# Scores in two PSUM banks with the last 128 keys of two heads in a common bank, four common banks instead of two, spread directly ahead of the values, and the first chunk's split moved into the attention

## The chip, the cores and the metric

The kernel runs on one core of one Trainium2 chip. The metric is the device time of one execution in microseconds. Engines: TensorE (PE), VectorE (DVE), ScalarE (ACT), GpSimd (POOL), and SyncE (SP), which issues most DMAs. Each engine executes its own instructions in a fixed order; semaphores make one wait for another. PSUM has eight banks of 512 float32 per partition.

## What is computed

```python
q_pool = q.reshape(B, H, S // 2, 2, D).mean(axis=3)      # B 2, H 8, S 1152, D 64
scores = q_pool @ k.transpose(0, 1, 3, 2) / sqrt(D)
attn = exp(scores - max(scores)); attn /= attn.sum(-1) + 1e-9
x = (attn @ v)                                           # as 1152 tokens x 512
x = softplus(x @ w_in) @ w_out                           # d_ff 2048
out = max(x @ w1, x @ w2, x @ w3) @ w_out2               # d_ff 768
```

The dense weights arrive as float64 and are turned to float32 on the chip. Where a product must be more exact than one float32r matmul, an operand is split into a high and a low part, and two or three matmuls are summed.

## The kernel before, in words

The sixteen heads are worked on in eight pairs (`pr`). A pair has 1152 keys and 576 pooled queries a head: four query tiles of 128 for each head (`t` 0 to 3, `i` the head) and one tile that holds the last 64 queries of both heads, nine tiles in all (`one_tile`, L588).

One tile goes through five steps. `scores` (L437) fills a score tile of three PSUM banks, 384 keys in each, with two matmuls a bank (three for the ninth tile). `key_max` (L453) takes the negated maximum of all 1152 scores on DVE. `exps` (L459) makes the exponentials on ACT with that maximum as bias, in one instruction, and its accumulator gives the row's sum. `turn_e` (L472) transposes them on PE, 3 x 128 keys at a time, into one of two common banks, and `keep_e` (L478) copies that bank to SBUF as `p`, on ACT or DVE as the table `ENGINE` says (D or A for each third of each tile). There are two score tiles, six banks, and two common banks (`NTB`). The common banks also serve the transposes of k and q for the next pair (`turn_k`, `turn_q`), the spread inverses and the values.

After four (or five) tiles `finish` (L614) adds the second half: `inverse` (L496) makes 1 / sum on DVE, `spread` (L505) turns it along the columns on PE, `keep_spread` (L530) copies it to `rr` on ACT, `values` (L518) multiplies p by v in 36 matmuls, and `divide` (L541) multiplies both into `xy` on DVE.

The order of all this is not the order of the code. `Order` (L47) collects every step with an engine, a cost, a place, what it reads and writes, and whether it takes or frees a common bank. `ordered` then plays the steps through with those costs, always taking on an engine the step with the lowest place that could start, and the result is the instruction order of every engine. Places are the tile's number plus an offset from the table `AT` or, for the next pair's preparation, `PREP`. Ten dense weights are prepared in gaps of the last pairs (`load_weight` on SP, `size_weight` on ACT, `bound_weight` on POOL, `float_weight` in three steps on DVE, `high_weight` on ACT, `low_weight` on DVE).

The dense part has an `Order` of its own (L692), on seven of the eight banks, over three chunks of 384 tokens. `halves_x` (L875) splits a chunk: `high_x` (L783) casts on ACT and `low_x` (L786) subtracts on POOL, in four pieces. `up` (L714) is one projection of 12 matmuls; `size_h`, `lost1`, `lost2`, `log_h`, `lost3`, `soft`, `high_g`, `low_g` make the softplus and its split on ACT, DVE and POOL; `down` (L760) follows four projections later. Line names in the trace: s is a score tile, nm the negated maximum, te the transposed exponentials, tk and tq transposed k and q, tr the spread inverses, x under L522 the values, bank_h, bank_y, bank_o the dense banks.

Of the kernel before, what the change touches and what calls it, by code (L numbers as in the profile page):

```python
# [124 lines left out]
def kernel(  # L130
# [52 lines left out]
    xy = xpool.tile([P, NC, NTOK], F32, tag="xy", name="xy")  # L183
    pools = {"pre": wpre}
# [252 lines left out]
    def scores(m, pr, i, t, b):  # L437
        if b == 0:
            tiles["s", m] = ps.tile([P, NB, 512], F32, tag=slot("s", m, NS), name=f"s_{m}")
        sp = tiles["s", m]  # L440
        q1, q2, k1, kl = q1s[pr % 2], q2s[pr % 2], tiles["k1", pr], tiles["kl", pr]
        cols = slice(b * BK, (b + 1) * BK)
        to = sp[:, b, :BK]
# [9 lines left out]
    def key_max(m):  # L453
        tiles["nm", m] = sm.tile([P, 1], F32, tag=slot("nm", m, 3), name=f"nm_{m}")
# [4 lines left out]
    def exps(m, w, x, first):  # L459
        e = pp.tile([P, S], F32, tag=slot("e", m, NE), name=f"e_{m}")  # L460
        if first:
            tiles["sum", w] = sm.tile([P, 5], F32, tag=slot("sum", w, 2), name=f"sum_{w}")
        nc.scalar.activation(  # L463
            out=e.rearrange("p (b s) -> p b s", b=NB),
            in_=tiles["s", m][:, :, :BK],
            func=AF.Exp,
            bias=tiles["nm", m],
            accum_out=tiles["sum", w][:, x : x + 1],
        )
        tiles["e", m] = e  # L470
# [22 lines left out]
    def width(w):  # L493
        return 2 * QB if w % 2 == 0 else 2 * QB + TAILQ

    def inverse(w):  # L496
# [3 lines left out]
        nc.vector.tensor_scalar(  # L500
            out=r[:, :nx], in0=tiles["sum", w][:, :nx], scalar1=1e-9, scalar2=None, op0=ALU.add
# [28 lines left out]
    def keep_spread(w, n):  # L530
        rr = sm.tile([P, 2 * QB + TAILQ], F32, tag="rr", name=f"rr_{w}")
        tiles["rr", w] = rr
        nc.scalar.copy(rr[:, : width(w)], tiles["t", n])

    def token_cols(w):
# [3 lines left out]
        return c, slice(t0, t0 + width(w))  # L539

    def divide(w, n):  # L541
        c, cols = token_cols(w)
        nc.vector.tensor_tensor(
            out=xy[:, c, cols], in0=tiles["t", n], in1=tiles["rr", w][:, : width(w)], op=ALU.mult
        )

    counts = {"t": 0}
    TILES = 2 * NT + 1

# [37 lines left out]

    def one_tile(pr, x):  # L588
        i, t = (x % 2, x // 2) if x < 2 * NT else (0, NT)
        m = TILES * pr + x  # L590
        w = 2 * pr + (t >= 2)
# [3 lines left out]
        banks = [f"{s}_{b}" for b in range(NB)]  # L595
        for b in range(NB):
            order.add("PE", 0.35 if t < NT else 0.52, m + b / NB, scores, m, pr, i, t, b,
                      reads=[f"q{z}{y}_{g}" for z in (1, 2) for g in range(2)]
                      + [f"q1{y}_d0", f"q1{y}_d1", f"k1{y}_0{b}", f"k1{y}_1{b}", f"kl{y}_{b}"],
                      writes=(banks[b],) + ((s,) if b == 0 else ()))  # L600
        order.add("DVE", 1.28, m + AT["max"], key_max, m, reads=banks + [s], writes=(slot("nm", m, 3),))
        order.add("ACT", 1.21, m + AT["exp"], exps, m, w, sx, sx == 0,
                  reads=[slot("nm", m, 3), s] + banks, writes=(e, f"sum{w % 2}"))
        for b in range(NB):
            n, p = next_bank(), m + AT["turn"] + b / NB
            engine = ENGINE[sx][b]
            order.add("PE", 0.33, p, turn_e, m, b, n, reads=(e, "pw"), writes=(f"b{n}",), take=("t", n))
# [6 lines left out]
    def finish(m, w):  # L614
        nx = 4 if w % 2 == 0 else 5
        y = (w // 2) % 2
        at = m + AT["values"]
        n1, n2 = next_bank(), next_bank()
        order.add("DVE", 0.3, m + 0.3, inverse, w, reads=(f"sum{w % 2}",), writes=(f"r{w % 2}",))
        order.add("PE", 0.6, m + AT["spread"], spread, w, n1, reads=(f"r{w % 2}",), writes=(f"b{n1}",), take=("t", n1))  # L620
        order.add("ACT", 0.36, m + AT["spread"], keep_spread, w, n1, reads=(f"b{n1}",), writes=("rr",), free=("t", n1))
        order.add("PE", 4.0 if w % 2 == 0 else 4.9, at, values, w, n2,
                  reads=[f"p_{x}_{b}" for x in range(nx) for b in range(NB)] + [f"v{y}"],
                  writes=(f"b{n2}", "pw"), take=("t", n2))
        order.add("DVE", 0.4, at - 3, divide, w, n2, reads=(f"b{n2}", "rr"), free=("t", n2))
# [40 lines left out]
    FIRST = (2, 3, 4, 5, 6, 7, 1)  # L666
# [13 lines left out]
    def tok(ch):  # L680
        return slice(ch * TOK, (ch + 1) * TOK)


    xs = {}
    for ch in reversed(range(NCH)):
# [97 lines left out]
    def high_x(ch, c):  # L783
        nc.scalar.copy(xs[0, ch][:, c], xy[:, c, tok(ch)])

    def low_x(ch, c):  # L786
        nc.gpsimd.tensor_tensor(
            out=xs[1, ch][:, c],
# [209 lines left out]
```

## Time and profile before

| | us |
|---|---|
| median of 3 runs (lowest, highest) | 676.99 (676.8, 677.45) |
| span of the profiled execution | 675.7 |
| difference of the median to that span | 1.3 |
| PE matmul busy in it | 637.5 (94%) |
| PE weight loads busy | 556.3 (82%) |
| DVE, ACT, POOL busy | 446.9, 351.5, 219.6 |

For the profiled execution the profile gives the span, from its first to its last instruction; some 1.3 us lie around it, as the third line has it. Busy shares are means over stages that have different limits: the attention runs to about 308.8 us, the dense layers from there to the end. A matmul's row ends when its last result is modelled to have left the array, so the rows of neighbours overlap, and the distance of their starts tells what one costs.

### The profile page before, as it was taken

Reading aid. Unit: us, or ns where it says so; the run is one execution under the profiler, and the core shown is the slowest. Engines: PE = TensorE matmul, PEld = TensorE weight load, DVE = VectorE, ACT = ScalarE, POOL = GpSimd, SP = SyncE. Lnnn points to the kernel's source line nnn. Section 1 sums busy time; section 2 is a strip of 40 time slices with the busy share of each in tenths; the row PEclk is TensorE's granted clock in tenths of the full one; section 3 lists DMA queues with packets and bytes.
Section 4 is the critical chain, followed back from the end, with each engine's and each line's share of the span. In section 5 each row is a group of like instructions: output and inputs, shape, how many; then the busy total and the mean of one; then the engine's idle time right before and its main releaser. Section 6 shows DMA issues by size and latency. Waiting matters only on the chain.

```text
span 675.7 us, 10352 instructions
## 1 busy us (share of the span) xinstructions
PE 637.5 (94%) x3914; PEld 556.3 (82%) x3914; DVE 446.9 (66%) x747; ACT 351.5 (52%) x697; POOL 219.6 (32%) x204
## 2 busy tenths in 40 slices
PE   2899999999999998999899999999999999999997
PEld 1676677676767766667799999999999999999996
DVE  3866667667777799985867979797688871111111
ACT  4655555556565666656767676767574431211211
POOL 1100000000000112216987877779695510000000
PEclk9999999999999999999799999999999999999999
DMA  7443433324241735212223333232022310100101
GB/s 191 107 105 89 96 98 73 100 69 98 68 99 43 198 116 164 94 64 81 76 63 97 122 98 122 94 126 93 32 94 95 124 32 1 47 1 1 47 1 48
DMA packets 56546, 56.87 MB, mean 84 GB/s; under 512 B 21168, under 2 KB 47792, under 8 KB 56496
## 3 DMA queue, kind: packets, MB, share of 16 engines
q1 hardware_dynamic: 55280, 55.62, 28.8%
q10 hardware_dynamic: 1216, 0.59, 0.3%
q8 instruction: 31, 0.51, 0.3%
q14 instruction: 19, 0.16, 0.1%
HBM read 43.52 MB, written 2.36 MB: 68 GB/s over the span
## 4 chain that ended last, share of the span: by engine, by line
PE 78%; DVE 10%; ACT 6%; issue 2%; DMA 2%; POOL 2%; SPq 0%; ACTq 0%; DVEq 0%; POOLq 0%
PE bank_h_m L675 17%; PE bank_h L675 15%; PE bank_y L675 14%; PE x L522 9%; PE te L476 7%; PE bank_o L675 6%; DVE nm L455 4%; PE s L446 4%; ACT e L463 4%; DVE p L491 3%; PE s L447 3%; DMA k<-in_k_dram 2%; ACT p L489 1%; PE tk L348 1%; PE s L449 1%
## 5 line engine op out<-in xcount | busy, mean ns | idle before, releaser
L226 POOL TENSOR_SCALAR size<-size 128x512 f32<-128x512 f32 x56 | 84.3, 1507 | 98.9 <-ACT size L221 98.7
L675 PE MATMUL bank_h_m<-x,wh 128*128 128x384 f32 x432 | 114.6, 339 | 0.0
L476 PE MATMUL te<-ident,e 128*128 128x128 f32 x648 | 101.8, 282 | 11.2 <-DVE p L491 7.8
L455 DVE TENSOR_REDUCE nm<-s 128x1 f32<-128x1152 f32 x72 | 97.4, 1352 | 14.7 <-PE s L447 12.5
L675 PE MATMUL bank_h<-x,wh 128*128 128x384 f32 x384 | 106.3, 339 | 0.2 <-DVE gl L757 0.2
L476 PEld LDWEIGHTS te<-ident,e 128*128 128x128 f32 x648 | 73.1, 140 | 38.8 <-DVE p L491 20.1
L463 ACT ACTIVATE e<-s,nm 128x1152 f32<-128x1152 f32 x72 | 88.3, 1226 | 22.0 <-DVE nm L455 17.0
L675 PEld LDWEIGHTS bank_h_m<-x,wh 128*128 128x128 f32 x432 | 78.9, 188 | 0.8
L446 PE MATMUL s<-k,q 128*128 128x384 f32 x192 | 76.1, 396 | 3.1 <-ACT e L463 3.1
L489 ACT COPY p<-te 128x384 f32<-128x384 f32 x88 | 39.7, 482 | 72.0 <-PE te L476 71.8
L491 DVE COPY p<-te 128x384 f32<-128x384 f32 x128 | 66.5, 552 | 11.7 <-PE te L476 9.9
L522 PE MATMUL x<-p,v 128*64 128x320 f32 (+1 forms) x576 | 73.3, 408 | 0.0
L675 PE MATMUL bank_h_m<-x,wl 128*128 128x384 f32 x216 | 73.1, 338 | 0.0
L675 PEld LDWEIGHTS bank_h<-x,wh 128*128 128x128 f32 x384 | 70.3, 188 | 1.1 <-DVE gl L757 0.6
L675 PE MATMUL bank_y<-gh,wh 128*128 128x384 f32 x192 | 66.1, 344 | 3.7 <-ACT gh L752 3.7
L333 POOL TENSOR_TENSOR qs<-q 128x512 f32<-128x512 f32 x7 | 8.9, 1273 | 185.7 <-PE tq L401 166.5
L675 PE MATMUL bank_y<-gl,wh 128*128 128x384 f32 x192 | 65.9, 343 | 0.1
L675 PE MATMUL bank_y<-gh,wl 128*128 128x384 f32 x192 | 65.8, 343 | 0.0
L447 PE MATMUL s<-kl,q 128*128 128x384 f32 x192 | 65.4, 341 | 0.0
L675 PE MATMUL bank_h<-x,wl 128*128 128x384 f32 x192 | 65.0, 339 | 0.0
L522 PEld LDWEIGHTS x<-p,v 128*64 128x64 f32 x576 | 39.9, 137 | 28.2 <-issue 2.3
L733 POOL TENSOR_TENSOR d<-e,d 128x384 f32<-128x384 f32 x48 | 49.0, 1022 | 29.1 <-DVE d L726 26.5
(216 smaller groups left out, 1096.9 us busy)
## 6 DMA issues: line engine op xcount, KB each, us to landing
raw<-in_moe_w_out_dram SPq DMA_DIRECT2D x22, 512.0 KB, 3.3
raw<-in_moe_w_dram SPq DMA_DIRECT2D x18, 512.0 KB, 3.5
raw<-in_moe_w_in_dram SPq DMA_DIRECT2D x16, 512.0 KB, 3.8
k<-kh SPq DMA_DIRECT2D x28, 288.0 KB, 5.8
k<-in_k_dram SPq DMA_DIRECT2D x16, 288.0 KB, 4.5
v<-in_v_dram SPq DMA_DIRECT2D x16, 288.0 KB, 3.2
q<-in_q_dram SPq DMA_DIRECT2D x14, 256.0 KB, 3.2
out_dram<-ob SPq DMA_DIRECT2D x9, 256.0 KB, 2.0
```

What stands on the lines that cost most here:

```text
L226: nc.gpsimd.tensor_scalar(out=size, in0=size, scalar1=SMALLEST, scalar2=None, op0=ALU.max)
L333: engine.tensor_tensor(out=qs.rearrange("p t i d -> p i t d"), in0=q1[:, :, :, 0], in1=q1[:, :, :, 1], op=ALU.add)
L446: nc.tensor.matmul(to, q1[:, i, at1 : at1 + QB], k1[:, i, cols], start=True, stop=False)
L447: nc.tensor.matmul(to, q2[:, at2 : at2 + QB], kl[:, cols], start=False, stop=True)
L455: nc.vector.tensor_reduce(out=tiles["nm", m], in_=tiles["s", m][:, :, :BK], axis=AX.XY, op=ALU.max, negate=True)
L463: nc.scalar.activation(out=e.rearrange("p (b s) -> p b s", b=NB), in_=tiles["s", m][:, :, :BK], func=AF.Exp, bias=tiles["nm", m], accum_ou ...
L476: nc.tensor.transpose(tp[:, t], tiles["e", m][:, j * P : (j + 1) * P], ident)
L489: nc.scalar.copy(to, tp)
L491: nc.vector.tensor_copy(to, tp)
L522: nc.tensor.matmul(x[halves(i)], tiles["v", w // 2][:, i, j], tiles["p", w, j // KT][:, i, j % KT, : width(w)], start=(j == 0), stop=(j == ...
L675: nc.tensor.matmul(ps, lhs(a, kk), rhs(bb, kk), start=start and n == 0, stop=stop and n == last)
L733: nc.gpsimd.tensor_tensor(out=d, in0=gs["e", i], in1=d, op=ALU.subtract)
```

## The change

- A score tile has two banks of 512 keys (`SB`). The last 128 keys of both heads of a query tile go to one common bank, `rest_scores`, and have their own maximum, `rest_max`; `key_max` takes the maximum of the 1024 and then the minimum of the two negated maxima. `exps` covers 1024 keys and `rest_exps` the last 128; each accumulates its own sum, and `inverse` adds the two.
- The freed two banks become common banks: `NTB` is 4.
- The spread is placed directly ahead of the values and waits for the same copies; `rr` has two buffers.
- For chunk 0 the casts and subtractions of `halves_x` are made in the attention, one piece after each of the first four pairs; its two tiles are allocated at the start.
- The tables `AT`, `ENGINE` and `PREP` have new numbers, and the planner's costs are those of the new steps. The dense part takes its banks in another order (`FIRST`).

```diff
-NTB = 2
+NTB = 4
-AT = {"max": -1.78, "exp": -0.31, "turn": 0.93, "keep": 0.1, "spread": 4.0, "values": 5.26}
-ENGINE = ["DAA", "DDD", "DAA", "DDA", "ADD"]
-PREP = {1: -5.28, 2: -7.74, 3: -4.5, 4: -3.31, 5: -1.64}
+SB = 512
+AT = {"rest": -0.7, "max": 2.3, "exp": -0.95, "turn": 1.03, "keep": -0.1, "values": 4.27}
+ENGINE = ["DAA", "DAD", "DAA", "DAD", "ADA"]
+PREP = {1: -2.9, 2: -10.61, 3: -7.52, 4: -3.98, 5: -5.52}
...
+    def scores(m, pr, i, t, b):
+        if b == 0:
+            tiles["s", m] = ps.tile([P, NM, SB], F32, tag=slot("s", m, NS), name=f"s_{m}")
+        score(tiles["s", m][:, b], pr, i, t, slice(b * SB, (b + 1) * SB))
+
+    def rest_scores(w, pr, t, n):
+        tp = bank(n, [P, heads(t), NR], f"sr_{w}")
+        for i in range(heads(t)):
+            score(tp[:, i], pr, i, t, slice(NM * SB, S))
+
+    def rest_max(w, t, n):
+        tiles["nr", w] = sm.tile([P, 2], F32, tag=slot("nr", w, 2), name=f"nr_{w}")
         nc.vector.tensor_reduce(
-            out=tiles["nm", m], in_=tiles["s", m][:, :, :BK], axis=AX.XY, op=ALU.max, negate=True
-        )
+            out=tiles["nr", w][:, : heads(t)], in_=tiles["t", n], axis=AX.X, op=ALU.max, negate=True
+        )
+
+    def key_max(m, w, i):
+        nm = sm.tile([P, 2], F32, tag=slot("nm", m, 3), name=f"nm_{m}")
+        nc.vector.tensor_reduce(out=nm[:, 1:], in_=tiles["s", m], axis=AX.XY, op=ALU.max, negate=True)
+        nc.vector.tensor_tensor(out=nm[:, :1], in0=nm[:, 1:], in1=tiles["nr", w][:, i : i + 1], op=ALU.min)
+        tiles["nm", m] = nm[:, :1]
...
+    def rest_exps(m, w, sx, i, n):
+        nc.scalar.activation(
+            out=tiles["e", m][:, NM * SB :],
+            in_=tiles["t", n][:, i],
+            func=AF.Exp,
+            bias=tiles["nm", m],
+            accum_out=tiles["sum", w][:, 1, sx : sx + 1],
+        )
...
+        if i == 0:
+            n = rests[u] = next_bank()
+            p = m + AT["rest"]
+            order.add("PE", 0.44 if t < NT else 0.33, p, rest_scores, u, pr, t, n,
+                      reads=qs + ks(NM * SB, S), writes=(f"b{n}",), take=("t", n))
+            order.add("DVE", 0.3 if t < NT else 0.2, p, rest_max, u, t, n, reads=(f"b{n}",), writes=(f"nr{u % 2}",))
...
+        order.add("ACT", 0.31, m + AT["exp"], rest_exps, m, w, sx, i, n, reads=[nm, f"b{n}"],
+                  writes=(e + "r", f"sum{w % 2}"), free=("t", n) if i == heads(t) - 1 else None)
...
-        order.add("PE", 0.6, m + AT["spread"], spread, w, n1, reads=(f"r{w % 2}",), writes=(f"b{n1}",), take=("t", n1))
-        order.add("ACT", 0.36, m + AT["spread"], keep_spread, w, n1, reads=(f"b{n1}",), writes=("rr",), free=("t", n1))
+        order.add("PE", 0.7 if w % 2 == 0 else 0.9, at - 0.01, spread, w, n1, reads=[f"r{w % 2}"] + ready,
+                  writes=(f"b{n1}",), take=("t", n1))
+        order.add("ACT", 0.4, at - 3, keep_spread, w, n1, reads=(f"b{n1}",), writes=(f"rr{w % 2}",), free=("t", n1))
...
+        if w % 2 and w // 2 < NC:
+            order.add("ACT", 0.46, at, high_x, 0, w // 2, reads=(f"x{w - 1}", f"x{w}"), writes=(f"xh{w}",))
+            order.add("POOL", 1.1, at, low_x, 0, w // 2, reads=(f"xh{w}",))
...
-        if f == 0:
-            halves_x(ch, at - 6 if i else -100)
+        if f == 0 and i:
+            halves_x(ch, at - 6)
```

The new tables move instructions on every engine. Two places show it. The first is PE in a steady pair, behind the shorter value block (the last six of its 18 matmuls stand in the first row; s is a score tile, te a third of the transposed exponentials of one tile). Before:

```order
L522 MATMUL x_1140<-p_2_1011,v_662 64x256 x6
L476 MATMUL te_0_1169<-ident,e_1052 128x128 x3
L449 MATMUL s_1126<-k_2_799,q_0_97 128x384
L450 MATMUL s_1126<-k_2_799,q_0_97 128x384
L451 MATMUL s_1126<-kl_735,q_0_98 128x384
L476 MATMUL te_1_1179<-ident,e_1052 128x128 x3
L476 MATMUL te_2_1185<-ident,e_1052 128x128 x3
L476 MATMUL te_0_1193<-ident,e_1080 128x128 x3
L476 MATMUL te_1_1199<-ident,e_1080 128x128 x3
L476 MATMUL te_2_1205<-ident,e_1080 128x128 x3
L476 MATMUL te_0_1209<-ident,e_1112 128x128 x3
L476 MATMUL te_1_1217<-ident,e_1112 128x128 x3
```

In the changed kernel the transposes behind the same block, from the fifth row behind it on, read (sr is the common bank of the rest scores):

```order
L494 MATMUL te_2_1265<-ident,e_1153 128x128 x3
L494 MATMUL te_0_1272<-ident,e_1184 128x128 x3
L494 MATMUL te_1_1278<-ident,e_1184 128x128 x3
L443 MATMUL s_1282<-k_2_799,q_0_99 128x512
L444 MATMUL s_1282<-k_2_799,q_0_99 128x512
L445 MATMUL s_1282<-kl_611,q_0_100 128x512
L494 MATMUL te_2_1294<-ident,e_1184 128x128 x3
L494 MATMUL te_0_1300<-ident,e_1245 128x128 x3
L443 MATMUL sr_1305<-k_2_799,q_0_99 128x128
L444 MATMUL sr_1305<-k_2_799,q_0_99 128x128
L445 MATMUL sr_1305<-kl_611,q_0_100 128x128
```

Before, nine groups of transposes, seven of which stand here, follow one another with no score matmul between; now two or three groups alternate with half a score tile or a rest tile.

The second place is ACT at the junction of attention and dense layers: rr is the last copy of spread inverses, x the cast halves of a chunk (x_0, x_1, x_2 in the first block are chunks 0, 1, 2), wh and size belong to weights, e and u to the softplus of the first projection. Before:

```order
L533 COPY rr_3176<-tr_3150 128x320
L784 CAST x_0_3209<-xy 128x384 x4
L784 CAST x_1_3207<-xy 128x384
L265 CAST wh_3224<-t_3212 128x512
L221 ACTIVATE size_3227<-raw_3059 128x512
L784 CAST x_1_3207<-xy 128x384 x3
L784 CAST x_2_3205<-xy 128x384 x3
L265 CAST wh_3259<-t_3232 128x512
L221 ACTIVATE size_3262<-raw_3222 128x512
L784 CAST x_2_3205<-xy 128x384
L720 ACTIVATE e_3282<-bank_h_3242 128x384
L721 ACTIVATE e_3282<-e_3282 128x384
```

In the changed kernel:

```order
L555 COPY rr_3450<-tr_3424 128x320
L572 CAST x_1_3481<-xy 128x384 x4
L572 CAST x_2_3479<-xy 128x384
L261 CAST wh_3522<-t_3497 128x512
L768 ACTIVATE e_3525<-bank_h_3483 128x384
L769 ACTIVATE e_3525<-e_3525 128x384
L785 ACTIVATE u_3532<-e_3525 128x384
L217 ACTIVATE size_3550<-raw_3403 128x512
```

The casts of chunk 0 are gone from here, and the softplus of the first projection stands behind one weight cast instead of two weight casts, two sizes and seven casts of x that follow the fifth.

## Rows read from the trace of the kernel before

**Rows 1.** Windows: span, busy us (instructions) of PE, PEld, DVE, ACT, POOL; clock, DMA.
```profile
38.20:76.00 37.80, 35.29 (x251) 26.34 (x250) 25.72 (x39) 19.82 (x40) 1.68 (x2) 1.00 0.36 87
...
183.03:218.59 35.56, 34.18 (x246) 25.44 (x245) 24.71 (x38) 19.88 (x38) 1.68 (x2) 1.00 0.32 76
218.59:255.97 37.38, 34.72 (x249) 25.92 (x248) 31.58 (x51) 24.46 (x47) 6.28 (x5) 1.00 0.57 156
255.97:288.99 33.02, 30.62 (x223) 22.55 (x222) 32.62 (x54) 21.61 (x41) 8.80 (x6) 1.00 0.41 117
288.99:303.82 14.83, 13.35 (x104) 9.30 (x104) 11.80 (x20) 8.41 (x16) 3.37 (x2) 1.00 0.20 72
...
308.80:331.00 22.20, 18.17 (x88) 16.84 (x87) 18.48 (x31) 15.70 (x33) 17.30 (x17) 0.85 0.30 96
```

**Rows 2.** Critical chain: start us, us, what ran.
```profile
...
183.10 4.04 PE x L522 x36
199.70 5.00 PE x L522 x36
...
506.81 2.12 PE bank_h L675 x12
...
540.71 2.11 PE bank_o L675 x9
```

**Rows 3.** Timeline of PE, 187 to 199 us: start us, us, instruction.
```profile
187.98 0.84 PE L476 MATMUL te<-ident,e 128*128 128x128 f32 x6
...
191.49 1.67 PE L476 MATMUL te<-ident,e 128*128 128x128 f32 x9 [0.19 <-DVE p L491]
192.91 0.42 PE L446 MATMUL s<-k,q 128*128 128x384 f32 x1
...
193.59 0.42 PE L446 MATMUL s<-k,q 128*128 128x384 f32 x1
...
194.27 0.42 PE L446 MATMUL s<-k,q 128*128 128x384 f32 x1
```

**Rows 4.** Lines of DVE, 183.03 to 218.59 us: busy us, mean ns, idle before.
```profile
L455 DVE TENSOR_REDUCE nm<-s 128x1 f32<-128x1152 f32 x9 | 12.2, 1352 | 2.0 <-PE s L447 2.0
L491 DVE COPY p<-te 128x384 f32<-128x384 f32 x16 | 8.3, 552 | 1.4 <-PE te L476 1.1
...
L543 DVE TENSOR_TENSOR xy<-x,rr 128x320 f32<-128x320 f32 x1 | 0.5, 493 | 2.4 <-PE x L522 2.4
L543 DVE TENSOR_TENSOR xy<-x,rr 128x256 f32<-128x256 f32 x1 | 0.4, 425 | 3.0 <-PE x L522 3.0
...
L503 DVE RECIPROCAL r<-r 128x4 f32<-128x4 f32 x1 | 0.2, 178 | 0.0
```

**Rows 5.** Lines of ACT, the same stretch.
```profile
L463 ACT ACTIVATE e<-s,nm 128x1152 f32<-128x1152 f32 x9 | 11.0, 1223 | 3.1 <-DVE nm L455 2.8 <-PE te L476 0.2
L489 ACT COPY p<-te 128x384 f32<-128x384 f32 x11 | 4.9, 480 | 10.9 <-PE te L476 10.9
L463 ACT ACTIVATION_READ_ACCUMULATOR e<-s,nm 128x1 f32 x9 | 1.8, 195 | 0.0
...
L417 ACT ACTIVATE q<-tq 64x64 fp32r<-64x64 f32 x2 | 0.4, 211 | 0.0
```

**Rows 6.** Timeline of all engines, 308.9 to 324 us.
```profile
311.01 0.70 DVE L250 SCALAR_TENSOR_TENSOR t<-raw,t 128x512 int32<-128x512 int32 x1
...
312.80 2.57 ACT L784 CAST x<-xy 128x384 fp32r<-128x384 f32 x6
...
316.80 0.50 ACT L720 ACTIVATE e<-bank_h 128x384 f32<-128x384 f32 x1
...
323.29 0.69 PE L675 MATMUL bank_y<-gh,wh 128*128 128x384 f32 x1 [3.67 <-ACT gh L752]
```

**Rows 7.** Timeline of PE, 324 to 332 us.
```profile
324.91 0.52 PE L675 MATMUL bank_y<-gh,wh 128*128 128x384 f32 x1
325.23 0.52 PE L675 MATMUL bank_y<-gh,wl 128*128 128x384 f32 x1
```

More of the change, by code (lines that the diff above doesn't have):

```diff
@@ L183 @@
     xy = xpool.tile([P, NC, NTOK], F32, tag="xy", name="xy")
+    xs = {(z, 0): xpool.tile([P, NC, TOK], F32R, tag=f"x{z}0", name=f"x_{z}_0") for z in range(2)}
     pools = {"pre": wpre}
@@ L435, in both_q, with score @@
         nc.sync.dma_start(q1[D:, 1, TAILQ:], q2[D:, NQ:])
[L437 to L440, printed above, removed]
+    NM = S // SB
+    NR = S - NM * SB
+    def score(to, pr, i, t, cols):
         q1, q2, k1, kl = q1s[pr % 2], q2s[pr % 2], tiles["k1", pr], tiles["kl", pr]
-        cols = slice(b * BK, (b + 1) * BK)
-        to = sp[:, b, :BK]
         if t < NT:
@@ L463, in exps @@
+    def exps(m, w, sx):
+        tiles["e", m] = pp.tile([P, S], F32, tag=slot("e", m, NE), name=f"e_{m}")
+        if sx == 0:
+            tiles["sum", w] = sm.tile([P, 2, 5], F32, tag=slot("sum", w, 2), name=f"sum_{w}")
         nc.scalar.activation(
-            out=e.rearrange("p (b s) -> p b s", b=NB),
-            in_=tiles["s", m][:, :, :BK],
+            out=tiles["e", m][:, : NM * SB].rearrange("p (b s) -> p b s", b=NM),
+            in_=tiles["s", m],
             func=AF.Exp,
             bias=tiles["nm", m],
-            accum_out=tiles["sum", w][:, x : x + 1],
+            accum_out=tiles["sum", w][:, 0, sx : sx + 1],
@@ L499, in inverse @@
         tiles["r", w] = r
-        nc.vector.tensor_scalar(
-            out=r[:, :nx], in0=tiles["sum", w][:, :nx], scalar1=1e-9, scalar2=None, op0=ALU.add
+        s = tiles["sum", w]
+        nc.vector.scalar_tensor_tensor(
+            out=r[:, :nx], in0=s[:, 0, :nx], scalar=1e-9, in1=s[:, 1, :nx], op0=ALU.add, op1=ALU.add
         )
@@ L530, in keep_spread, with divide @@
     def keep_spread(w, n):
-        rr = sm.tile([P, 2 * QB + TAILQ], F32, tag="rr", name=f"rr_{w}")
+        rr = sm.tile([P, 2 * QB + TAILQ], F32, tag=slot("rr", w, 2), name=f"rr_{w}")
         tiles["rr", w] = rr
         nc.scalar.copy(rr[:, : width(w)], tiles["t", n])
-    def token_cols(w):
+    def divide(w, n):
         pr, half = divmod(w, 2)
@@ L538, in token_cols @@
         t0 = b * NQ + half * 2 * QB
[L539 to L542 removed]
         nc.vector.tensor_tensor(
[L544 removed]
+            out=xy[:, c, t0 : t0 + width(w)], in0=tiles["t", n], in1=tiles["rr", w][:, : width(w)], op=ALU.mult
         )
@@ L548, with tok, high_x, low_x @@
     TILES = 2 * NT + 1
+    def tok(ch):
+        return slice(ch * TOK, (ch + 1) * TOK)
+    def high_x(ch, c):
+        nc.scalar.copy(xs[0, ch][:, c], xy[:, c, tok(ch)])
+    def low_x(ch, c):
+        nc.gpsimd.tensor_tensor(
+            out=xs[1, ch][:, c],
+            in0=xy[:, c, tok(ch)],
+            in1=xs[0, ch][:, c].bitcast(F32),
+            op=ALU.subtract,
+        )
     def next_bank():
@@ L606, in one_tile @@
             engine = ENGINE[sx][b]
-            order.add("PE", 0.33, p, turn_e, m, b, n, reads=(e, "pw"), writes=(f"b{n}",), take=("t", n))
+            order.add("PE", 0.33, p, turn_e, m, b, n, reads=(e, "pw") + ((e + "r",) if b == NB - 1 else ()),
+                      writes=(f"b{n}",), take=("t", n))
             order.add("ACT" if engine == "A" else "DVE", 0.38 if engine == "A" else 0.45, m + AT["keep"] + b / NB,
@@ L678, in matmul3 @@
                 n += 1
[L680 to L685, printed above, removed]
+    for ch in reversed(range(1, NCH)):
         for z in range(2):
```

54 lines of the change are left out of this document (23 added, 31 removed).

## The prediction

> **What bounds the kernel now.** I read the windows first, stage by stage, because the attention (0 to 308.8 us) and the dense layers behind it have different limits. From 331 us to the end TensorE never pauses in the chain of waits: an up-projection of 12 matmuls of 384 columns takes 2.12 us and an output group of 9 matmuls of 512 columns 2.11 us [rows 2], that is 0.177 and 0.234 us a matmul. The change does not touch that work, so I leave its 345 us alone.
>
> In the attention one pair of heads repeats every 35.6 us [rows 1] (the stretch from 183.03 us), and PE is "busy" for 34.2 of it. That figure hides waits, since a matmul's modelled end covers some 0.2 us after it. I therefore compare the pair's content with its period. Per pair: 57 score matmuls at 0.177 (10.1 us); 90 transposes of e and k. Their price comes from two neighbouring score starts, 193.59 and 194.27 us, between which lie two score matmuls and three transposes [rows 3]: (0.68 - 0.353) / 3 = 0.109 us each, 9.8 us in all; the two value blocks 4.04 and 5.00 us [rows 2]; and about 2 us for transposed q and for the spread inverses (my estimate from their count at the transposes' price). Together 30.9 us, so **about 4.6 us of a pair are waits**. Where they are is seen after the shorter value block: 27 transposes from 187.98 to the next score at 192.91 us [rows 3] take 4.93 us for 2.9 us of work, ending on DVE's and ACT's copies of p, which alone free the two common banks.
>
> VectorE is the second limit. It is busy 24.7 of 35.6 us [rows 1], and it also stands still 2.4 + 3.0 us in front of the two divides, which wait for the values [rows 4]: in its fixed order nothing passes them. That makes 30.1 us, almost PE's 30.9. In the last stretch (218.59 to 303.82, 85.2 us) it also prepares ten weights and is busy 31.6 + 32.6 + 11.8 = 76.0 us [rows 1]: there it is the limit.
>
> At the junction, 308.8 to 331 us, PE runs 88 matmuls in 22.2 us at a mean clock of 0.85 [rows 1]. At 0.177 they are worth 15.6 us, so **6.6 us are lost**. PE finishes five projections, then stands 3.67 us until the first split g is there [rows 6]; behind the pause matmuls start 0.32 us apart [rows 7] instead of 0.177, which is the 1.2 GHz level in place of 2.4.
>
> **The change part by part.**
>
> *Scores, PE.* Out go 456 matmuls of 384 columns (192 + 192 + 72), 80.6 us; in come 304 of 512 columns at 0.234, 71.1 us, and 152 of 128 columns. The trace has no float32r matmul that short. Lower end: the step from 512 to 384 columns is 0.057, so two more steps give 0.062. Upper end: a 384-column one, 0.177. I take 0.109, because the transposes load and move the same 128 by 128: 16.6 us. PE's content grows by 7.1 us, 0.9 per pair (ends: 0 and +17.4 in all). A weight load lies under each, so the added loads cost nothing beyond that price.
>
> The Trainium skill (TensorE: Matmul & The Clock Gate, Back-to-back issue gap) gives about 81 ns for a stream of loads and matmuls at 128 columns. The transposes here need 109. With 81 the term would be 4.3 us smaller.
>
> *DVE per pair.* Nine maxima get 128 columns shorter: the divides give (493 - 425) / 64 = 1.06 ns a column [rows 4], so -1.2 us. Five maxima over the rest banks cost like the 256-column divide, 0.425, or less: +2.0. Nine minima over one element cost 0.178 like the reciprocal [rows 4], and each waits for the maximum right before it, so I take 0.22: +2.0. The new table gives DVE 13 copies in place of 16 (2 x (1+2+1+2) + 1): 3 x 0.55, -1.6. Sum +1.2, to 25.9 us; with the 5.4 us in front of the divides 31.3, against a PE content of 31.8. The minimum holds up the copies and maxima behind it on DVE; the exponential and with it te wait for it.
>
> *ACT per pair.* Nine second exponentials: 64 columns take 211 ns, and (1223 - 211) / 1088 = 0.93 ns a column gives 0.27, plus an accumulator read of 0.195 [rows 5], less 0.12 on the first: +3.1. Three more copies at 0.48: +1.4. A high half for chunk 0 in four pairs, +0.5: behind the divide, with p copies queued behind it, some 0.2 us late. ACT rises from 19.9 [rows 1] to 24.9 us of the period; it stays off the bound as a sum. By the Trainium skill (ScalarE: Activation LUTs, What ACT_TABLE_LOAD costs) an activation with a per-partition bias has some 280 ns fixed, which makes the second one 0.39 instead of 0.27; ACT would then need 1.1 us more per pair.
>
> *Four common banks.* This is what the added work buys. The rest scores hold one bank for about two tiles, so te has three, at moments two. The transposes are also laid out with score blocks between them, as the order shows. Ends for the 4.6 us of waits: all stay (period 36.5), or none (31.8). With DVE's 31.3 close beside PE's 31.8, and each engine in a fixed order, the two will not interleave without gaps; I take half, 2.3, so a period of 34.1: **1.5 us less**, times the five pairs from 38.20 to 218.59: -7.5. Spread and values as one block move the spread behind the copies: 1 us of PE that is there anyway; its copy to rr lies under the values. No price.
>
> *Last stretch.* Over its 19 tiles DVE changes by 19 x (0.22 - 0.14) + 11 x 0.4 - 6 x 0.55 = +2.6, to 78.6; of the 9.2 us it stood idle I let 4.6 remain: **-2** (ends 0 and -4.5). On SP two more raw weights now stand ahead of pair 7's v and k copies, each waiting for a slot that DVE frees; the copies are needed a pair later, so I price it at nothing, and at 1 to 3 us if DVE is late. The start, to 38.2 us, I leave as it is (one us either way).
>
> *First halves early.* Chunk 0's four casts and four subtractions leave the junction. Their place on ACT is taken by chunk 1's, and ACT reaches the first softplus right behind one weight cast. That cast waits for DVE's last float step, 311.01 + 0.70 [rows 6]; 0.6 later, at 312.3, the softplus starts, where now it starts at 316.80 behind six casts [rows 6]. The chain from there to the first down matmul is 323.29 - 316.80 = 6.5 us, so it is ready at 318.8, before the five projections end (308.8 + 5 x 2.12 = 319.4). The pause goes, and with it the slow clock. Next in line is POOL, for the second and third g; I leave 0.5 us. **-6.2**. POOL's subtractions in the attention cost nothing: it is busy 1.7 of 35.6 us [rows 1].
>
> *Sum:* -7.5 - 2 - 6.2 = -15.7. The profiled span is 675.7; 1.3 us around it make the median of 676.99, and I carry them over. **661 us.**
>
> **Rivals.**
> 1. *More of the waits goes.* With three or four banks te never waits, and the small matmuls run nearer their lower end: period 32.4, -16, last stretch -4, junction -6.5: 650 us. For it: the waits of the pair mostly end on p copies. Against: DVE at 31.3. The page's 81 ns points the same way.
> 2. *The small matmuls cost 0.177.* Then 10 us come back: 671.
> 3. *The junction does not do what it says*, since POOL or DVE take ACT's place ahead of the first g: 667. Against: the operations of POOL and DVE for that g are counted in the 6.5 us chain as it stands.
> 4. *Slower: the tile's own chain becomes the bound.* Rest maximum, maximum, minimum, two exponentials: some 0.7 us longer for each tile, on a DVE that may not pass a divide, while two rest banks at once leave te the two it has now. All 4.6 us of waits stay, PE's +0.9 comes on top, and small matmuls near their upper end add 1.3: period 37.8, times 7.4 pairs +16, less 6.2: 687. It decides once the period passes 36.4 us, where the junction's gain is used up.
>
> **How the numbers follow.** Forecast (656 to 666) 0.52, rival 1 0.16, rival 2 0.13, rival 3 0.09, rival 4 0.10. Range 652 to 673: it takes in the forecast and rivals 2 and 3, and the nearer half of rival 1. A measurement of this kernel tells about 0.2%, 1.4 us, from no change; faster 0.87, within 0.03 (a mild form of rival 4), slower 0.10.
>
> **What would show it.** In the changed profile: starts of the value blocks 34.1 us apart per pair; the 128-column matmuls spaced near 0.11 us; PE's wait for p copies halved; DVE busy about 26 us per pair and the last stretch 83 us long; the first down matmul with no pause before it and a granted clock of 1.00 from the attention's end on. A period over 36.4 us, a pause of over 3 us at the junction, or a spacing of 0.17 would prove it wrong at that step.

## The result, and the profile of the changed kernel

The changed kernel takes **653.5 us** (median of 4 runs, 653.0 to 653.79) against 677.2 us of the kernel before on the same chip: a ratio of 0.9648, 95% interval 0.9634 to 0.9661. The forecast was 661, with a range of 652 to 673: the sign and the range held, the size was 7.5 us short. The span of the profiled execution fell from 675.7 to 650.9 us. By the starts of the value blocks it divides so:

| stretch | before, us | after, us | difference | forecast |
|---|---|---|---|---|
| start to the first value block | 38.20 | 36.13 | -2.1 | 0 |
| five pairs | 180.4 | 165.1 | -15.3 | -7.5 |
| to the start of the last value block | 85.2 | 83.2 | -2.0 | -2 |
| from there to the end | 371.9 | 366.4 | -5.5 | -6.2 |
| span | 675.7 | 650.9 | -24.8 | -15.7 |

The median now stands 2.6 us above the span of the profiled execution, where I had carried over 1.3; so 9.1 us of miss in the span are 7.5 in the time. Of the five pairs the first fell by 4.8 us (from 37.80 [rows 1] to 32.98), the other four by 2.6 us each.

The windows of the changed kernel answer to [rows 1]: stretch, its length, busy us and instructions of PE, PEld, DVE, ACT and POOL, granted clock, DMA share and rate. The first two are pairs, the next three the last stretch, the sixth the junction.

```profile
36.13:69.11 32.98, 32.85 (x246) 24.82 (x245) 24.47 (x49) 23.28 (x61) 2.69 (x4) 1.00 0.22 57
135.01:167.99 32.98, 32.86 (x246) 24.83 (x245) 24.43 (x50) 23.51 (x61) 2.69 (x4) 1.00 0.42 100
201.27:236.55 35.28, 33.94 (x246) 24.56 (x247) 31.06 (x61) 26.61 (x66) 6.67 (x6) 1.00 0.58 150
236.55:269.90 33.35, 32.10 (x235) 23.24 (x232) 32.22 (x63) 25.29 (x61) 7.99 (x5) 1.00 0.40 116
269.90:284.51 14.61, 13.25 (x104) 9.54 (x105) 14.29 (x28) 12.15 (x30) 3.40 (x2) 1.00 0.30 91
289.40:312.00 22.60, 20.72 (x117) 19.99 (x116) 20.49 (x35) 16.20 (x34) 17.48 (x17) 1.00 0.30 94
```

A pair now takes 32.98 us instead of 35.56. To see where the 2.6 us went I add up, over one pair, the distance from each matmul's start to the next, by what the first of the two computes (a wait counts with the matmul ahead of it):

| per pair, us | before | after |
|---|---|---|
| scores (three banks before, two after) | 12.24 | 10.35 |
| rest scores | - | 2.12 |
| transposed exponentials, 81 | 10.63 | 8.34 |
| values, 72 | 9.04 | 9.04 |
| transposed q, k, spread | 3.66 | 3.14 |
| sum | 35.57 | 32.99 |

The scores as a whole grew by 0.2 us, the transposes lost 2.3: 131 ns each before, 103 now. (103 is less than the 109 from one transpose to the next, because at a change to scores some 0.08 us move from the last transpose to the second score; the last section has the numbers.) The timeline of PE (start us, us, instruction) shows how it looks:

```profile
145.07 0.49 PE L494 MATMUL te<-ident,e 128*128 128x128 f32 x3
145.32 0.48 PE L440 MATMUL s<-k,q 128*128 128x512 f32 x1
145.63 0.40 PE L441 MATMUL s<-kl,q 128*128 128x512 f32 x1
145.87 0.23 PE L440 MATMUL sr<-k,q 128*128 128x128 f32 x1
145.93 0.27 PE L441 MATMUL sr<-kl,q 128*128 128x128 f32 x1
146.04 0.28 PE L440 MATMUL sr<-k,q 128*128 128x128 f32 x1
146.15 0.28 PE L441 MATMUL sr<-kl,q 128*128 128x128 f32 x1
146.26 0.84 PE L494 MATMUL te<-ident,e 128*128 128x128 f32 x6
146.86 0.48 PE L440 MATMUL s<-k,q 128*128 128x512 f32 x1
```

None of these rows has a wait, where [rows 3] had blocks of transposes that waited for a copy of p. Between 145.93 and 146.26 us the 128-column matmuls start 0.11 us apart; the 0.06 ahead of them stand at the change from 512 columns.

The profile's own list of PE's waits says the same for the attention as a whole (us in total, times, longest). The first two lines are the kernel before (38 to 303 us), the other two the changed one (36 to 284 us):

```profile
PE te L476 <- DVE p L491: 7.5, 24, 1.2
PE te L476 <- ACT p L489: 2.6, 9, 0.3
```

```profile
PE te L494 <- ACT p L513: 1.4, 3, 0.9
PE te L494 <- DVE p L515: 1.1, 3, 0.4
```

That is 10.1 us of waits for copies of p before and 2.5 now; I had forecast that they would halve. The list starts to count a wait only at the modelled end of the matmul ahead of it, so the start distances show more of each. The lines of DVE and of ACT in the pair from 135.01 us (busy us, mean ns, idle before) answer to [rows 4, 5]. DVE:

```profile
L465 DVE TENSOR_REDUCE nm<-s 128x1 f32<-128x1024 f32 x10 | 12.1, 1213 | 0.4 <-PE s L441 0.2
L515 DVE COPY p<-te 128x384 f32<-128x384 f32 x13 | 6.9, 551 | 1.1 <-PE te L494 0.9
L459 DVE TENSOR_REDUCE nr<-sr 128x2 f32<-128x256 f32 x4 | 1.7, 416 | 0.2 <-PE sr L441 0.2
...
L466 DVE TENSOR_TENSOR nm<-nm,nr 128x1 f32<-128x1 f32 x9 | 1.4, 161 | 0.3
...
L561 DVE TENSOR_TENSOR xy<-x,rr 128x320 f32<-128x320 f32 x1 | 0.5, 492 | 3.9 <-PE x L544 3.9
...
L561 DVE TENSOR_TENSOR xy<-x,rr 128x256 f32<-128x256 f32 x1 | 0.4, 424 | 2.4 <-PE x L544 2.4
```

ACT:

```profile
L473 ACT ACTIVATE e<-s,nm 128x1024 f32<-128x1024 f32 x9 | 10.1, 1118 | 1.2 <-DVE nm L466 1.1
L513 ACT COPY p<-te 128x384 f32<-128x384 f32 x14 | 6.7, 479 | 5.4 <-PE te L494 5.3
L482 ACT ACTIVATE e<-sr,nm 128x128 f32<-128x128 f32 x9 | 3.3, 362 | 0.0
```

DVE is busy for 24.4 us and stands 6.3 us in front of the two divides; the other 2.2 us lie in small gaps. In front of its maxima it stood 2.0 us a pair waiting for scores [rows 4], now 0.4.

The junction, from the timeline of all engines, answers to [rows 6, 7]:

```profile
292.73 0.50 ACT L768 ACTIVATE e<-bank_h 128x384 f32<-128x384 f32 x1
...
298.15 1.59 POOL L222 TENSOR_SCALAR size<-size 128x512 f32<-128x512 f32 x1
299.72 1.01 POOL L790 TENSOR_TENSOR d<-u,d 128x384 f32<-128x384 f32 x1
300.00 0.34 PE L728 MATMUL bank_y<-gh,wh 128*128 128x384 f32 x1
...
303.26 0.45 PE L728 MATMUL bank_y<-gh,wh 128*128 128x384 f32 x1 [1.51 <-DVE gl L805]
```

The first softplus starts 3.2 us after the first projection (289.49), where it took 8.0 (316.80 against 308.8). The first down matmul follows the five projections without a pause, and the granted clock is 1.00 throughout. What is left is a shorter pause of 1.5 us behind nine matmuls, for the second g.

### The profile page after: what moved, and what is told of

Same layout as the page of the kernel before. It is cut to its first block, busy times and chain, and to the rows that moved or that the text cites. A ratio compares the mean times of both kernels' runs of the same rounds, so it can differ in the third digit from the quotient of the medians.

```text
span 650.9 us, 10574 instructions
## 1 busy us (share of the span) xinstructions
PE 626.8 (96%) x3914; PEld 548.4 (84%) x3914; DVE 445.7 (68%) x835; ACT 377.0 (58%) x865; POOL 220.4 (34%) x204
## 4 chain that ended last, share of the span: by engine, by line
PE 52%; POOL 1%; DVE 1%; issue 0%; ACT 0%; DVEq 0%; ACTq 0%
PE bank_h_m L728 17%; PE bank_y L728 15%; PE bank_h L728 14%; PE bank_o L728 6%; POOL size L222 0%; POOL d L781 0%; POOL d L790 0%; POOL x L575 0%; DVE d L774 0%; DVE t L246 0%; DVE t L242 0%; DVE t L233 0%; DVE wl L266 0%; ACT wh L261 0%; ACT ob L862 0%
## 5 line engine op out<-in xcount | busy, mean ns | idle before, releaser
L494 PE MATMUL te<-ident,e 128*128 128x128 f32 x648 | 93.8, 277 | 3.2 <-ACT p L513 1.4
L473 ACT ACTIVATE e<-s,nm 128x1024 f32<-128x1024 f32 x72 | 80.5, 1119 | 17.2 <-DVE nm L466 16.2
L465 DVE TENSOR_REDUCE nm<-s 128x1 f32<-128x1024 f32 x72 | 87.4, 1214 | 3.7 <-PE s L441 2.8
L513 ACT COPY p<-te 128x384 f32<-128x384 f32 x112 | 52.9, 479 | 37.0 <-PE te L494 36.3
L440 PE MATMUL s<-k,q 128*128 128x512 f32 x128 | 60.1, 470 | 1.6 <-ACT e L473 1.6
L515 DVE COPY p<-te 128x384 f32<-128x384 f32 x104 | 55.2, 550 | 5.8 <-PE te L494 4.7
L575 POOL TENSOR_TENSOR x<-xy,x 128x384 fp32r<-128x384 f32 x24 | 24.1, 1026 | 91.0 <-ACT x L572 91.0
L843 DVE TENSOR_TENSOR mg<-bank_h_m,mg 128x384 f32<-128x384 f32 x18 | 10.0, 556 | 61.6 <-PE bank_h_m L728 61.6
```

Source lines behind the costliest of these rows:

```text
L440: nc.tensor.matmul(to, q1[:, i, at1 : at1 + QB], k1[:, i, cols], start=True, stop=False)
L465: nc.vector.tensor_reduce(out=nm[:, 1:], in_=tiles["s", m], axis=AX.XY, op=ALU.max, negate=True)
L473: nc.scalar.activation(out=tiles["e", m][:, : NM * SB].rearrange("p (b s) -> p b s", b=NM), in_=tiles["s", m], func=AF.Exp, bias=tiles["nm ...
L513: nc.scalar.copy(to, tp)
L515: nc.vector.tensor_copy(to, tp)
L575: nc.gpsimd.tensor_tensor(out=xs[1, ch][:, c], in0=xy[:, c, tok(ch)], in1=xs[0, ch][:, c].bitcast(F32), op=ALU.subtract,)
```

## The experiments

### The parts of the change, one at a time

**Three common banks.** Only the number changes, and the eighth PSUM bank stays empty.

```diff
-NTB = 4
+NTB = 3
```

> The changed kernel with three common banks instead of four, the eighth PSUM bank unused; the tables stay. Theory (the four banks took the waits away): the rest scores hold one bank, at moments two, so the transposes are back at the two banks of the kernel before, or one, while PE has 0.2 to 0.9 us more work in a pair; period 35.5 us or more instead of 33.0, value blocks of one pair at least 35 us apart, and PE's waits for p copies back at 7 us or more; 653.5 + 7.4 x 2.5 = 672 us or above. Rival (the new tables and the new shares of DVE and ACT did it, the banks are only where the work stands): period under 34 us, 661 us or less.

701.2 us, ratio to the kernel before 1.0348 (1.0333 to 1.0364), 39.5 us a pair. The columns are those of the windows above; then PE's waits in the attention (42 to 319 us): us in total, times, longest.

```profile
141.50:181.00 39.50, 35.38 (x245) 24.66 (x244) 25.19 (x49) 23.50 (x61) 2.67 (x3) 1.00 0.37 83
```

```profile
PE te L494 <- ACT p L513: 11.2, 28, 0.8
PE s L440 <- ACT e L473: 7.2, 19, 0.6
PE te L494 <- DVE p L515: 4.1, 11, 0.9
```

With one bank held by the rest scores the transposes have two, as before, and wait 15.3 us for p copies (ACT and DVE together), against 10.1 in the kernel before and 2.5 in the changed one. So two-bank score tiles with three common banks and these tables lose: this is the direction of rival 4, and larger than its 687. The planner lays the steps out anew for three banks, with tables that were made for four, so the 47.7 us to the changed kernel are not the bank's alone. The order of the changed kernel, kept as it is on three banks, was not run.

**The first halves back at the junction**, the rest as changed.

```diff
-        if w % 2 and w // 2 < NC:
-            order.add("ACT", 0.46, at, high_x, 0, w // 2, ...)
-            order.add("POOL", 1.1, at, low_x, 0, w // 2, ...)
...
-        if f == 0 and i:
-            halves_x(ch, at - 6)
+        if f == 0:
+            halves_x(ch, at - 6 if i else -100)
```

> The changed kernel with the casts and subtractions of chunk 0 back in front of the dense layers. Theory (the junction's gain comes from ACT reaching the first softplus behind one cast): the attention keeps its period of 33.0 us, the first softplus starts some 4 us later after the first dense matmul, PE stands some 3.5 us before the first down matmul; 653.5 + 5 = 658 to 660 us. Rival (POOL and the late g's set the junction now, and the casts would be hidden): 653 to 655 us.

660.1 us, 0.9739 (0.9725 to 0.9754): 6.6 us are lost, as the theory had it but for 0.1 us. In the timeline the six casts are back in front of the softplus, and PE's pause with them:

```profile
295.79 2.57 ACT L572 CAST x<-xy 128x384 fp32r<-128x384 f32 x6
...
300.43 0.48 ACT L765 ACTIVATE e<-bank_h 128x384 f32<-128x384 f32 x1
...
306.96 0.44 PE L725 MATMUL bank_y<-gh,wh 128*128 128x384 f32 x1 [4.28 <-ACT gh L797]
```

From the last value block's start to the end it takes 371.6 us instead of 366.4: 5.2 of the 6.6 us (7.7 in the profiled execution) are the junction. The rest is in the attention, which I had expected to stay as it is: its pairs take 33.3 us instead of 33.0, and one takes 34.4, with a wait of 0.9 us for a load of q.

**The first halves early in the kernel before**, and nothing else (the same edit as the diff's `finish` and `add_up`, in the old code).

> The kernel before with chunk 0's casts and subtractions moved into the attention as the change does, and nothing else. Theory (this part's gain stands by itself): no pause of 3.67 us before the first down matmul; 677 - 5.5 = 671 to 672 us, the attention's period as before, 35.6 us. Rival (it needs the other parts, since POOL or DVE take ACT's place at the junction): 675 us or more.

671.4 us, 0.9901 (0.9885 to 0.9918). From the last value block to the end 366.6 us instead of 371.9, and the pair keeps its 35.60 us. In the timeline of PE the pause of 3.67 us [rows 6] has become 1.73, later, for the second g:

```profile
319.15 0.34 PE L693 MATMUL bank_y<-gh,wh 128*128 128x384 f32 x1
...
322.62 0.44 PE L693 MATMUL bank_y<-gh,wh 128*128 128x384 f32 x1 [1.73 <-DVE gl L771]
```

This part stands by itself: 5.3 us here, 5.2 us in the run before.

**All three tables of the kernel before in the changed kernel.**

```diff
-AT = {"rest": -0.7, "max": 2.3, "exp": -0.95, "turn": 1.03, "keep": -0.1, "values": 4.27}
-ENGINE = ["DAA", "DAD", "DAA", "DAD", "ADA"]
-PREP = {1: -2.9, 2: -10.61, 3: -7.52, 4: -3.98, 5: -5.52}
+AT = {"rest": -0.7, "max": -1.78, "exp": -0.31, "turn": 0.93, "keep": 0.1, "values": 5.26}
+ENGINE = ["DAA", "DDD", "DAA", "DDA", "ADD"]
+PREP = {1: -5.28, 2: -7.74, 3: -4.5, 4: -3.31, 5: -1.64}
```

> The changed kernel with the numbers of the kernel before in the three tables (places of maximum, exponential, transposes, copies and values, the shares of DVE and ACT, the next pair's preparation); spread and values stay one block. DVE has 16 copies in a pair again, about 1.6 us more. Theory (the banks carry the gain, the tables a smaller part): period 33.5 to 34.5 us, 657 to 665 us. Rival (the tables carry it): period 35.5 us or more, 672 us or above. If the tables are nothing: 654 us.

691.2 us, 1.0209 (1.0181 to 1.0237): **slower than the kernel before**, although it has four common banks and no pause before the first down matmul. A pair takes 38.6 us. The theory as I had written it, banks first and tables a smaller part, fell. Four more runs ask for the tables' share.

### Which of the tables

Each of the next three has one line of the diff above and leaves the other two as changed; the fourth puts the new numbers into the kernel before, with its spread at 4.26.

Old `ENGINE`:

> The changed kernel with the old table of shares alone: DVE makes 16 p copies in a pair, ACT 11 (changed kernel: 13 and 14). Theory (the places decide, DVE has room): DVE 24.4 + 1.6 busy and 6.3 us in front of the divides is 32.3 us, still under the period of 33.0; period 33 to 33.6 us, 653 to 659 us. Rival (DVE is the second bound and its share is what lost 38 us in the run with all three old tables): period 36 us or more, 675 us or above.

Old `AT`:

> The changed kernel with the old table of places alone: on DVE and ACT the maximum and the exponential of a tile come ahead of the copies of earlier tiles again (place -1.78 against +2.3 for the maximum), and spread and values a tile later. Theory (the places decide): most of the 38 us of the run with all three old tables, 675 to 692 us, period 36 us or more. Rival (the shares or the preparation decide): 654 to 664 us.

Old `PREP`:

> The changed kernel with the old places of the next pair's transposes of k and q alone. Theory (the places of the tiles decide, nine transposes and five others of 150 in a pair only need any gap): period 33 to 34 us, 653 to 661 us; the start may lose the 2 us that it gained. Rival (banks held by a transposed k or q that waits for ACT and DVE cost te its bank): period 35 us or more, 668 us or above.

New tables in the kernel before:

> The kernel before, two common banks and scores in three, with the new numbers in its three tables, the spread just ahead of the values; nothing else. Theory (neither banks nor tables gain alone): no gain, 677 us or above, period 35.6 us or more. Rival (the tables carry the gain by themselves): period about 33 to 34.5 us, 657 to 668 us.

| score tile and banks | tables | us | ratio to before (interval) | one pair, us |
|---|---|---|---|---|
| three banks, two common | old | 677.2 | 1 | 35.6 |
| three banks, two common | new | 701.7 | 1.0342 (1.031 to 1.0374) | 38.6 |
| two banks, four common | old, all three | 691.2 | 1.0209 (1.0181 to 1.0237) | 38.6 |
| two banks, four common | old shares only | 659.4 | 0.9734 (0.9719 to 0.9748) | 33.9 |
| two banks, four common | old places only | 684.1 | 1.0102 (1.0086 to 1.0118) | 37.4 |
| two banks, four common | old preparation only | 708.2 | 1.0468 (1.0432 to 1.0503) | 42 (33.8 to 46.3) |
| two banks, three common | new | 701.2 | 1.0348 (1.0333 to 1.0364) | 39.5 |
| two banks, four common | new | 653.5 | 0.9648 (0.9634 to 0.9661) | 33.0 |

The shares cost 6 us, just past the upper end of what was expected. The places cost 31 us, as expected of them. The old preparation, which I had expected to cost 8 us at most, costs 55, more than any other. And the new tables without the banks lose as well, as the theory of that run had it. With the tables at hand, then, neither half gains by itself; banks and order gain only together. The costs don't add: 6, 31 and 55 are 92 us, and all three old tables together cost 38. What one table is worth depends on the other two, so the 55 us are not the preparation's share of the gain.

What the preparation does can be read from PE's timeline in that run:

```profile
165.06 0.39 PE L445 MATMUL s<-kl,q 128*128 128x512 f32 x1
...
167.60 1.21 PE L494 MATMUL te<-ident,e 128*128 128x128 f32 x6 [0.27 <-DVE p L515]
168.65 0.53 PE L344 MATMUL tk<-ident,k 128*128 128x128 f32 x3
169.01 1.98 PE L494 MATMUL te<-ident,e 128*128 128x128 f32 x12
171.20 1.53 PE L494 MATMUL te<-ident,e 128*128 128x128 f32 x12 [0.21 <-ACT p L513]
...
174.81 0.52 PE L344 MATMUL tk<-ident,k 128*128 128x128 f32 x3 [1.29 <-DMA k<-in_k_dram]
```

The last third of the next pair's k is transposed at 168.65 us only; SP is done issuing its copies at 174.9, and they land between 175.9 and 179.8. From 165.3 to 180.8 us PE has no scores to put between the transposes; then the scores of a new pair come in one heap, and DVE and ACT, which had stood idle, are late for everything. The transposes of exponentials take 14.5 us of that pair, against 8.3. The instructions are the same ones; by this timeline the larger part of what is lost is their mixture, though no run restores the mixture alone. A smaller part is a plain wait for data: 1.3 us in this pair, for the load of a later pair's k (last row), and 9.0 us of such waits in the whole attention. In the run with old places PE's timeline shows single-kind blocks as well: 18 transposes in a row that take 3.4 us, from 156.27 to 159.69, for 2.0 us of work.

### What bounds a pair now

**Rest scores made twice**: 19 more matmuls of 128 columns in a pair, the order of all engines unchanged.

```diff
         for i in range(heads(t)):
-            score(tp[:, i], pr, i, t, slice(NM * SB, S))
+            for _ in range(2):
+                score(tp[:, i], pr, i, t, slice(NM * SB, S))
```

> The changed kernel with every 128-column score matmul made twice (the second pass starts its bank anew, so the result is the same); the planner's costs, and so every engine's order, stay. That adds 19 matmuls of 0.11 us, 2.1 us, to PE in a pair. Theory (PE's content is what the pair's period of 33.0 us now consists of, the waits are gone): period 35.1 us, and 653.5 + 7.4 x 2.1 = 669 us. Rival (waits on DVE or ACT are still in the period and swallow part of it): period under 34 us, 661 us or less.

664.1 us, 0.9811 (0.9796 to 0.9825), between the two. The pair grew by 1.53 us to 34.51, for 2.04 us of added matmuls (38 of 0.110 against 19): three quarters of an addition to PE reach the period, and some 0.5 us of waits still took the rest. PE's rows now fill the pair (34.51 of 34.51 us), so a pair of the changed kernel needs at most 34.51 - 2.04 = 32.5 us of PE's own time.

**Two more minima on DVE** behind each maximum, again with the order unchanged.

```diff
         nc.vector.tensor_tensor(out=nm[:, :1], in0=nm[:, 1:], in1=tiles["nr", w][:, i : i + 1], op=ALU.min)
+        nc.vector.tensor_tensor(out=nm[:, :1], in0=nm[:, :1], in1=tiles["nr", w][:, i : i + 1], op=ALU.min)
+        nc.vector.tensor_tensor(out=nm[:, :1], in0=nm[:, :1], in1=tiles["nr", w][:, i : i + 1], op=ALU.min)
```

> The changed kernel with two more one-element minima behind each maximum on DVE (they repeat the first; the result is the same); the order of every engine stays. That adds 18 instructions of 0.16 to 0.22 us, 2.9 to 4.0 us, to DVE in a pair, and 0.3 to 0.4 us to each tile's way from scores to exponential. Theory (only PE bounds the pair, DVE's 24.4 us busy leave it room): period 33 to 34 us in the steady pairs, the last stretch some 3 us longer since DVE is the limit there; 655 to 663 us. Rival (DVE is a second bound, as the prediction had it with its 31.3 us against PE's 31.8): period 35.5 us or more, 673 us or above.

674.9 us, 0.9966 (0.9953 to 0.9978): 21 us lost to 18 instructions of 0.16 to 0.18 us in a pair. The theory fell. The rival held, though its period of 35.5 us or more came out as 35.3. The windows of a pair and of the last stretch:

```profile
144.49:179.80 35.31, 34.15 (x245) 24.78 (x244) 27.32 (x68) 23.92 (x61) 2.69 (x4) 1.00 0.42 94
215.44:306.09 90.65, 80.58 (x580) 57.25 (x581) 84.83 (x192) 65.04 (x155) 17.69 (x14) 1.00 0.41 113
```

DVE became 2.9 us busier, and the period grew by 2.3; the stand in front of the divides shrank only from 6.3 to 5.4. DVE, busy for 74% of a pair of the changed kernel, has next to no room: what it stands idle before the divides cannot be used by anything behind them. The minima also lengthen each tile's way from scores to exponential, by 0.3 us, and that could be the cause instead. PE's waits speak for DVE's queue: in the attention PE stands 11.8 us for DVE's copies of p and its differences kl (changed kernel: 1.3), and only 1.0 us (0.7) for ACT's exponentials. The run with old shares points the same way, though in a new layout: 1.2 us more of copies on DVE, which lie behind the exponential, made the pair 0.9 us longer. So both engines bound the pair, and work added to either shows.

### A better version

**POOL's weight step later.** Two of POOL's steps are made to wait for a later softplus (its mark is `l` with the number).

```diff
-            work.add("POOL", 0.9, at - 1, bound_weight, n, writes=(f"size{n % 2}",))
+            work.add("POOL", 0.9, at - 1, bound_weight, n, reads=(f"l{n - 9}",) if n < NPRE + 4 else (), writes=(f"size{n % 2}",))
...
-        work.add("POOL", 1.1, at, lost3, i, reads=("u",), writes=(d,))
+        work.add("POOL", 1.1, at, lost3, i, reads=("u",), writes=(d, f"l{i}"))
```

> The changed kernel with POOL's step for the thirteenth and fourteenth weight held until the fourth and fifth softplus have passed POOL. Theory (the pause before the last quarter of the first down projection comes from the 1.59 us of that step between the two subtractions of the second softplus): that pause of 1.5 us goes, 651.5 to 652.5 us. Rival (the pause moves to the weight, or to the third softplus, which waits on POOL as well): 653 to 655 us.

652.6 us, 0.9639 (0.9626 to 0.9652). That is just above what the theory had. The pause is 0.50 us instead of 1.51:

```profile
302.12 0.45 PE L728 MATMUL bank_y<-gh,wh 128*128 128x384 f32 x1 [0.50 <-DVE gl L805]
```

From the last value block's start to the end it takes 365.1 instead of 366.4 us. The 1.3 us are seen there; in the whole time the intervals overlap. In the new layout another piece of POOL's work stands between the same two subtractions, 1.14 us of `low_x` from 298.03 us on; the half microsecond that stays may come from it.

**Two copies of a pair from DVE to ACT**, on top of it.

```diff
-                      keep_e, w, i, t, b, n, sx == 0, engine,
+                      keep_e, w, i, t, b, n, sx == 0, "A" if (sx, b) == (1, 2) else engine,
```

> The kernel of the run before this one (652.6 us), and of the 13 p copies that DVE makes in a pair two are made by ACT, at the same points of the order of all steps; the planner's costs stay, so nothing else changes its place. DVE has 1.1 us less in a pair, ACT 1.0 us more. Theory (DVE is the second bound of the pair and the limit of the last stretch): steady pairs fall from 33.0 to 32.5 us at most, since PE's own content is near 32.4, and the last stretch loses 2 us or more: 648 to 650.5 us. Rival (DVE and ACT wait for each other in a fixed order, and an ACT that comes later with its exponentials gives the gain back): 652 us or more.

652.1 us, 0.9623 (0.961 to 0.9637): the rival. Undisturbed pairs fall by 0.2 us to 32.76, and the last stretch stays at 83.3 us. In the profiled execution one of the five pairs is disturbed: it takes 34.3 us, with a wait of 1.3 us for a load of q, so that the five together took 165.7 us against 165.1. It is the fastest of all, but by no more than its interval from the run before; I don't call it better than that one.

## Why the prediction was right in sign and short in size

- **Content of PE: the difference right.** I counted 30.9 us before and 31.8 after. By start distances without a wait in between (scores 0.174 before and 0.232 after, transposes 0.109, rest scores 0.111) scores, rest scores and exponentials' transposes need 18.8 us before and 19.8 after: +1.0 for a forecast of +0.9. The level may be up to 0.7 too low on both sides: the run with the rest scores twice allows 32.5 us for the changed pair. The 0.109 for a 128-column score, between bounds of 0.062 and 0.177, was right to 0.002. The Trainium skill (TensorE: Matmul & The Clock Gate, Back-to-back issue gap) would have had 81 ns, and this kernel's rows decide against it.
- **Lost waits: the term that was mis-sized.** "I take half, 2.3" of 4.6 us a pair. With my own content 32.98 - 31.8 = 1.2 us are left: 3.4 went, not 2.3. (With 32.5 us of content, and 31.5 before, 3.6 of 4.1 went.) With the content's +0.9 or +1.0 that is the 2.6 us a pair that the windows show, instead of 1.5: 5.4 us in five pairs. Another 2.4 us of the five pairs' miss of 7.8 come mostly from the first one: it took 37.80 us before [rows 1], and I priced it as a steady pair of 35.6. With the start's 2.1, less 0.7 at the junction, that is the miss in the span, 9.1 us but for rounding. My reason was that DVE's 31.3 us and PE's 31.8 would not interleave without gaps, each in a fixed order. That DVE is a second bound is borne out: two more minima on it cost 2.3 us a pair. But PE and DVE do interleave with hardly a gap, in the order that came with the new tables.
- **The tables had no term.** I gave them a sum of copies on DVE, -1.6 us, and no price of its own for their places; that transposes now lie between score blocks stood only as a reason beside the banks. With any one table old a pair takes 33.9, 37.4 or 42 us (with the old shares three copies change their engine, otherwise the instructions are the same). That the time fell into my range was luck in this respect: "all stay", the worst end that I gave the waits, is 36.5 us a pair, and with the old places or the old preparation the change comes out slower than the kernel before. Four banks with an order that isn't made for them come near the numbers of rival 4, which I gave 0.10; that they do so by its mechanism, the tile's own longer chain, no run shows.
- **DVE and ACT: a little less than forecast.** DVE 24.4 us instead of 25.9: the minimum takes 0.161, not 0.22, and the rest maximum 0.416 and 0.280. ACT 23.5 instead of 24.9, although its second exponential takes 0.362 us where I had worked out 0.27 from a 64-column row; neighbouring rows overlap, so sums of durations are too high on both. For the second exponential alone the Trainium skill (ScalarE: Activation LUTs, What ACT_TABLE_LOAD costs) was nearer: the estimate from its figures was 0.39.
- **Last stretch: right**, -2.0. DVE is busy for 77.6 of its 83.2 us. There I had put 78.6 and 83.
- **Junction: right mechanism, residue too small.** -5.5 against -6.2; the early halves are 5.2 to 5.3 of it in both kernels. I left 0.5 us for POOL and the second and third g; the pauses for the second were 1.5 and 0.4 us. The run with POOL's weight step moved names the cause of the longer one: 1.59 us of that step between the two subtractions of the second softplus.
- **Start: missed**, -2.1 for a forecast of nothing. It ends at 35.8 to 36.4 us with the new places and preparation on four banks, at 38.1 with the old preparation, at 39.9 with the old places and at 42.9 with three banks; added work, too, lengthens it, to 38.5 (more minima) and 38.9 (rest scores twice). So it goes with tables, banks and content like the pairs; which of its steps gained, no run shows.
- **The rivals.** Rival 1 (more of the waits goes) is what happened: its period of 32.4 us was 0.6 too low, its 650 us 3.5 too low. Its second reason, cheaper small matmuls, did not come true. Rivals 2 and 3 fell by the 0.11 us and by the junction's missing pause.

Open stays whether other tables would bring the kernel on three common banks, or on two, as far: those runs show tables that were made for another number of banks. What is shown is that the new banks with the old tables, and the new tables with the old banks, are slower than the kernel before. The spread's new place and the dense part's other order of banks were not tried alone.

## What to carry to other kernels

When a change comes with a new order of the same work, price the order as a term of its own, with a range: here it was worth more than the work that was added or saved, and the same resource with the old order was a loss. Waits that "an engine in a fixed order will keep" can go almost wholly, as they did here, if the next stage's inputs are ready early enough that two kinds of work always lie side by side; look in the timeline for stretches with one kind only. An engine that is busy for three quarters of a period may have no room at all: idle time in front of a late operand in its queue counts as used, and only adding to it and taking from it shows how much. Here 2.9 us more on DVE cost 2.3 us a pair, and 0.8 us less gave back 0.2.

## What the runs showed of the hardware

- Float32r matmuls of 128 columns in a row start 0.110 to 0.111 us apart, and float32 transposes 0.108 to 0.109, while float32r scores of 512 columns start 0.23 apart and those of 384 0.174.
- At a change from transposes to scores the first score's start stands 0.028 us behind the last transpose's and the second score's 0.26 (384 columns) or 0.315 us (512) behind the first: 0.08 less and 0.08 more than within a block. So mixing the two kinds costs PE next to nothing.
- The exponential of 128 columns takes 0.362 us and that of 1024 columns 1.118, so 0.84 ns a column and some 0.25 us for an instruction, beside 0.2 us for each accumulator read; by these durations, splitting one exponential in two costs ACT 0.26 us and one more accumulator read (before, 1152 columns took 1.223 us).
